# Softcap attention, then a gated feed-forward layer, on one core: VectorE priorities, output copies on VectorE, and weights converted and split one unit further ahead

## Chip, core and metric

The kernel runs on one core of a Trainium2 chip. The metric is the device time of one execution in microseconds (us). TensorE is called PE in the profile, VectorE DVE, ScalarE ACT, GpSimd POOL; SP is SyncE, whose queue (SPq) issues almost all DMAs here.

## What is computed

Attention over 4 batches, 12 heads, 448 positions and 64 features per head, with scores capped by tanh, and then a gated layer whose weights come as 64-bit floats:

```python
def _attn_ref(q, k, v, cap):
    scores = np.matmul(q, k.transpose(0, 1, 3, 2)) / np.sqrt(q.shape[-1])
    scores = cap * np.tanh(scores / cap)
    attn = np.exp(scores - np.max(scores, axis=-1, keepdims=True))
    attn = attn / (np.sum(attn, axis=-1, keepdims=True) + 1e-09)
    return np.matmul(attn, v)

def _moe_ref(x, w_gate, w_val, w_out):   # x: 1792 x 768; w_gate, w_val: 768 x 1536; w_out: 1536 x 768
    gate = 1.0 / (1.0 + np.exp(-(x @ w_gate)))
    return (gate * (x @ w_val)) @ w_out
```

## The kernel before

**Split numbers.** Products are made of halves: a 32-bit value is split into a high part (rounded to the matmul's own format, `hi`, line 171) and a low part (the rest, `lo`, line 180, a subtraction on VectorE at L182), and a product takes three matmuls: high by low, high by high, low by high.

**Attention** works on pairs of heads, numbered n = 0 to 23, six to a batch. `emit_T` (line 285) transposes q and k on TensorE (tiles tp), ScalarE takes the high part T out of PSUM (L176), VectorE the low part. `emit_S` (line 312) makes scores in four pieces sc and ScalarE's tanh takes each out of PSUM (L327); `emit_exp` is the exponential (L335). From pair 12 on, `emit_P` splits it (ph on ScalarE, pl and ph on VectorE) and GpSimd adds it up (tile a); `emit_PV` multiplies with v, and `emit_rd` (line 385) takes the two halves out of PSUM: tmp by ScalarE at L397, then VectorE joins them into xraw at L398. `emit_out` (line 400) divides: reciprocal at L416. Pairs 0 to 11 keep the exponential whole and have no join.

**The layer** runs batch by batch in `moe` (line 706). Weights are cut into 36 units of 128 x 768: units 0 to 23 are w_gate and w_val in three groups of four and four, units 24 to 35 w_out, six for each half t of the output's columns. Batch 0's product with units 0 to 23 makes tiles h (matmuls at L715); with the output units it makes three accumulators o{b}_{t}_0 to o{b}_{t}_2 (L791), 18 matmuls a unit. Accumulators and h share three PSUM buffers. At the end of each half the accumulators are copied into osb: 0 and 2 by VectorE (L804), 1 by ScalarE (L806), and stored.

**Conversion and split.** In batch 0 each unit is made from 64-bit words: `load_w64` (line 601, DMA at L603, a ring of three buffers), `convert_w` (line 606: ScalarE at L620, VectorE at L621, L622 and L623; two buffers in pair0) and `split_w` (line 650: high part by ScalarE at L176, low part by VectorE at L182, into one of four buffers wspl; stored to DRAM as wd at L659). Units 0 to 5 are made during the first six pairs. Later batches load the split units from DRAM (`load_to`, line 665, DMA at L671), into the same four buffers. What is made when is set in `next_w` (line 699), called as TensorE's next unit u is written down:

```python
    def next_w(u):
        if u < NU:
            convert_to(u + LEAD)
        split_w(u + AHEAD)
        load_to(u + WB)
        return w_spl.pop(u)
```

LEAD is 4 and AHEAD 2: with unit u, unit u + 3 is converted and u + 2 is split. A split writes the buffer of the unit four before it.

**The order of work.** TensorE and ScalarE run in the order in which the program writes them down (`manual_schedule`); pieces of attention for the next batch lie between the units. VectorE, GpSimd and SP are ordered by a scheduler, which `high_priority(offset)` tells to place an instruction as if it had been written that many instructions earlier. Only `emit_out`'s division had that before (`AHEAD_OF` is 400).

Of the kernel before, what the change touches and what calls it, by code (L numbers as in the profile page):

```python
# [23 lines left out]
AHEAD_OF = 400  # L24
# [191 lines left out]
def _bounded_attention(o, x_done):  # L216
# [14 lines left out]
    nc, c, ap = o.nc, o.c, o.ap  # L231
# [3 lines left out]
    B, H, S, D, NF, NC, R = o.B, o.H, o.S, o.D, o.NF, o.NC, o.REST  # L235
# [22 lines left out]
    def half(j):  # L258
        return slice(j * D, (j + 1) * D)
# [25 lines left out]
    def emit_T(n):  # L285

        if n >= NP:
            return
        t = qks.pop(n)
        ps = o.two_banks(f"tp{n}")  # L290
        if direct(n):
            o.transpose_evenly(ps[:, 0, :], t[:, 1])
        else:
            for m in range(NC):
                nc.tensor.transpose(
                    ps[:, 0, m * P:(m + 1) * P], t[:, 1, m].rearrange("p h d -> p (h d)"), ident
                )
        o.transpose_evenly(ps[:, 1, :], t[:, 0])
        T[n] = ap.tile([P, 2, 2, BANK], F32R, tag="T", bufs=1, name=f"T{n}")
        w = S if direct(n) else BANK  # L300
        hi, lo = T[n][:, 0, :, 0:w], T[n][:, 1, :, 0:w]
        if direct(n):
            parts = [(hi, lo, ps[:, :, 0:w])]
        else:
            parts = [tuple(
                x.rearrange("p i s -> p (i s)")[:, 0:BANK + S] for x in (hi, lo, ps)
            )]
        for a, b, x in parts:
            o.hi("a", a, x)
            o.lo("v", b, x, a)  # L310

    def emit_S(n, m):

# [65 lines left out]
    def row(n):  # L379
        b, p = divmod(n, o.NPAIR)  # L380
        if b not in x_raw:
            x_raw[b] = o.big.tile([P, o.NPAIR, S], F32, tag="xraw", name=f"xraw{b}")
        return x_raw[b][:, p, :]

    def emit_rd(n, j):

        if direct(n):
            if j == 0:
                rds[n] = ap.tile([P, S], F32, tag="rd", bufs=1, name=f"rd{n}")
            nc.scalar.activation(rds[n][half(j)], pvs[n, j][D:2 * D], AF.Copy)  # L390
            if not alone(n):
                nc.scalar.activation(row(n)[half(j)], pvs.pop((n, j))[0:D], AF.Copy)
        else:

            pv = pvs.pop((n, j))
            tmp = ap.tile([P, S], F32, tag="tmp", bufs=1, name=f"tmp{n}_{j}")
            nc.scalar.activation(tmp[half(j)], pv[D:2 * D], AF.Copy)  # L397
            nc.vector.tensor_add(row(n)[half(j)], pv[0:D], tmp[half(j)])  # L398

    def emit_out(n):  # L400
        b, p = divmod(n, o.NPAIR)
# [155 lines left out]
def _emit(tc, ctx, c, attention_of, q, k, v, w_gate, w_val, w_out, out):  # L557
    nc = tc.nc
    B, H, S, D = q.shape
# [7 lines left out]
    W64 = 3  # L567
    WRAW = 2
    KEEP = 3
    AHEAD = 2  # L570
    WB = 4
    GF = KF // NG

# [4 lines left out]
    o = _Ops(tc, ctx, c, q, k, v)  # L578
# [111 lines left out]
        flush_x()  # L690


    LEAD = 4

    R, NR, KR = o.REST, B * o.REST, 3
    assert NR % P == 0
# [9 lines left out]
    def moe(b):  # L706
        u0 = b * NU
        xs = x_spl[b]

        def passes(ps, s):  # L710
            for kk in range(KD):
                rh, rl = xs[:, 0, kk, :], xs[:, 1, kk, :]
                wh, wl = (s[:, i, kk * P:(kk + 1) * P] for i in range(2))
                for i, (a, r) in enumerate(((wh, rl), (wh, rh), (wl, rh))):
                    nc.tensor.matmul(  # L715
                        ps, a, r, start=(kk == 0 and i == 0), stop=(kk == KD - 1 and i == 2)
                    )
                if kk % 2 == 1:
                    yield 6

        g_spl = big.tile([P, 2, KF, S], F32R, tag="gspl", name=f"gspl{b}")
        rest = []
        if b == B - 1:
            tiles = []
            for tag, bufs, n in o.rest_tags:
                r = ap.tile([P, n, 2, KR, NR], F32R, tag=tag, bufs=bufs, name=f"rest{len(tiles)}")
                tiles += [r[:, i] for i in range(n)]
            for x, r in enumerate(tiles):
                for bb, d in enumerate(g_rest):
                    nc.sync.dma_start(  # L730
                        out=r[:, :, :, bb * R:(bb + 1) * R].bitcast(F32),
                        in_=d[:, :, x * KR:(x + 1) * KR, :].bitcast(F32),
                    )
                rest.append(r)
        u = u0
        for g in range(NG):
            gate = big.tile([P, GF, S], F32, tag="gate", name=f"gate{b}_{g}")
            for which in range(2):
                for j in range(GF):
                    f = g * GF + j  # L740
                    w = next_w(u)
                    u += 1
                    ps = ps_m.tile([P, S], F32, tag="m", name=f"h{b}_{which}_{f}")
                    yield from passes(ps, w)
                    gt = gate[:, j, :]
                    if which == 0:
                        nc.scalar.activation(gt, ps, AF.Copy)  # L747
                    else:
                        nc.vector.tensor_mul(gt, ps, gt)  # L749
                        o.hi("p", g_spl[:, 0, f, :], gt)  # L750
                        o.lo("v", g_spl[:, 1, f, :], gt, g_spl[:, 0, f, :])
                if which == 0:
                    nc.scalar.activation(gate, gate, AF.Sigmoid)  # L753
        moe1_done[b] = True
        flush_x()

        rest_cols = slice(o.FULL, S)
        chunks = [
            lambda i, k, at=m * P: g_spl[:, i, k, at:at + P] for m in range(o.NF)
        ]  # L760
        if b < B - 1:
            d = dram.tile([P, 2, KF, R], F32R, name=f"grest{b}")
            nc.sync.dma_start(out=d.bitcast(F32), in_=g_spl[:, :, :, rest_cols].bitcast(F32))
            g_rest.append(d)
        else:
            for x, r in enumerate(rest):
                for i in range(2):
                    nc.sync.dma_start(
                        out=r[:, i, :, b * R:].bitcast(F32),
                        in_=g_spl[:, i, x * KR:(x + 1) * KR, rest_cols].bitcast(F32),  # L770
                    )
            for at in range(0, NR, P):
                chunks.append(lambda i, k, at=at: rest[k // KR][:, i, k % KR, at:at + P])


        for t in range(2):
            acc = []
            for m in range(len(chunks)):
                if m < o.NF:
                    acc.append(ps_m.tile([P, HM], F32, tag="m", name=f"o{b}_{t}_{m}"))  # L780
                else:
                    acc.append(o.two_banks(f"o{b}_{t}_{m}")[:, 0, 0:HM])
            for x in range(0, KF, KU):
                w = next_w(u)
                u += 1
                for ps, g_of in zip(acc, chunks):
                    for kk in range(KU):
                        wh, wl = (w[:, i, kk * HM:(kk + 1) * HM] for i in range(2))
                        gh, gl = (g_of(i, x + kk) for i in range(2))
                        for i, (a, r) in enumerate(((gh, wl), (gh, wh), (gl, wh))):  # L790
                            nc.tensor.matmul(  # L791
                                ps, a, r, start=(x + kk == 0 and i == 0),
                                stop=(x + kk == KF - 1 and i == 2),
                            )
                    yield 3 * KU * HM / S
            to = out[:, t * HM:(t + 1) * HM]
            osb = big.tile([P, o.NF, HM], F32, tag="gate", name=f"osb{b}_{t}")
            for m, ps in enumerate(acc):
                if m == o.NF:
                    tag, bufs = o.out_tag  # L800
                    osb = ap.tile([P, NR // P, HM], F32, tag=tag, bufs=bufs, name=f"osr{b}_{t}")
                dst = osb[:, m % o.NF, :]
                if m % 2 == 0:
                    nc.vector.tensor_copy(dst, ps)  # L804
                else:
                    nc.scalar.activation(dst, ps, AF.Copy)  # L806
                if m == o.NF - 1:
                    nc.sync.dma_start(
                        out=to[b * S:b * S + o.FULL].rearrange("(m p) e -> p m e", p=P), in_=osb
                    )  # L810
            if b == B - 1:
                ends = to.rearrange("(b s) e -> b s e", s=S)[:, o.FULL:]
                for m in range(NR // P):
                    nb = P // R
                    nc.sync.dma_start(out=ends[m * nb:(m + 1) * nb], in_=osb[:, m, :])
# [7 lines left out]
    with tc.manual_schedule(engines=MS):  # L823
# [6 lines left out]
        for b in range(B):  # L830
            m = moe(b)
# [3 lines left out]
            while live_m or live_a:  # L835
                if live_a and (not live_m or done_a * tot_m <= done_m * tot_a):
                    n = next(att, None)
# [4 lines left out]
                else:  # L842
                    n = next(m, None)
# [34 lines left out]
```

## Time and profile before

| | us |
|---|---|
| median of 3 runs | 802.82 (801.18 to 804.92) |
| the profiled execution | 801.68, its span 799.9 |
| TensorE busy | 754.3 (94%) |
| TensorE weight loads busy | 646.6 (81%) |
| VectorE busy | 469.4 (59%) |
| ScalarE busy | 401.3 (50%) |
| GpSimd busy | 194.5 (24%) |
| mean granted TensorE clock | 0.979 |

Busy times are sums over the span; different stages have different limits, so what bounds the kernel is read stage by stage. The first stage (to 88 us) is attention of batch 0 alone. From 88 to 290 us batch 0's layer runs beside attention of batch 1, and all weights are converted; from 290 to 463 and 463 to 636 us batches 1 and 2 run beside the attention of the next; then batch 3's layer runs alone, until 787.5, and the last 12 us are the last output's way out.

### The profile page before, as it was taken

To read this page: it belongs to the slowest core of one execution; us is meant where nothing else is said; L and a number is where in the kernel's file an instruction comes from. 1 tells how busy PE (TensorE), PEld (TensorE's weight loads), DVE (VectorE), ACT (ScalarE), POOL (GpSimd) and SP (SyncE) were. 2 spreads that over 40 slices of the span, in tenths; PEclk is the share of its full clock that TensorE was granted. 3 is DMA by queue.
4 is the path that set the end of the run, shared out by engine and by line. 5 is a ranking of instruction groups with operands and counts; after the bars stand their busy time and mean duration, and the time that the engine had idled before them with its cause. 6 is when DMAs were issued, how large, how long until landed. Compare 5 with 4: busy or idle time off the path is not lost.

```text
span 799.9 us, 10153 instructions
## 1 busy us (share of the span) xinstructions
PE 754.3 (94%) x3908; PEld 646.6 (81%) x3908; DVE 469.4 (59%) x519; ACT 401.3 (50%) x421; POOL 194.5 (24%) x211
## 2 busy tenths in 40 slices
PE   7999799999998989999999999999979999999993
PEld 5554587888776878988899988887879999999993
DVE  1689349898799926768788628758797011211000
ACT  5898377886766428564764247664741020110000
POOL 1133101020130322524465215344452000100000
PEclk9999899999999989999999999999999999999997
DMA  8777547999989766555557866644378876665531
GB/s 225 179 216 219 181 143 243 363 298 329 289 241 395 246 255 195 179 172 181 174 183 243 276 201 182 193 158 158 127 227 252 289 239 233 211 225 191 180 107 53
DMA packets 133169, 172.99 MB, mean 216 GB/s; under 512 B 86136, under 2 KB 111224, under 8 KB 133112
## 3 DMA queue, kind: packets, MB, share of 16 engines
q1 hardware_dynamic: 132184, 172.02, 67.3%
q8 instruction: 33, 0.54, 0.3%
q10 hardware_dynamic: 928, 0.23, 0.1%
q14 instruction: 24, 0.20, 0.1%
HBM read 135.27 MB, written 36.18 MB: 214 GB/s over the span
## 4 chain that ended last, share of the span: by engine, by line
PE 68%; DVE 14%; ACT 8%; issue 4%; DMA 3%; POOL 1%; SPq 0%; DVEq 0%; POOLq 0%; ACTq 0%
PE h L715 32%; PE o L791 17%; PE pv L365 6%; PE sc L324 5%; DMA w<-in_moe_w_out_dram 2%; DVE pair L623 2%; PE tp L209 2%; ACT t L327 2%; DVE wspl L182 2%; PE pv L374 1%; ACT ph L176 1%; DVE rd L416 1%; PE pv L375 1%; DVE gspl L182 1%; ACT gate L753 1%
## 5 line engine op out<-in xcount | busy, mean ns | idle before, releaser
L715 PE MATMUL h<-xspl,wspl 128*128 128x448 f32 x1728 | 378.5, 373 | 0.0
L715 PEld LDWEIGHTS h<-xspl,wspl 128*128 128x128 f32 x1728 | 322.4, 189 | 42.4 <-issue 15.1
L791 PE MATMUL o<-wspl,gspl 128*128 128x384 f32 x864 | 164.4, 345 | 9.4 <-DVE wspl L182 5.3
L791 PEld LDWEIGHTS o<-wspl,gspl 128*128 128x128 f32 x864 | 154.5, 193 | 14.9 <-DVE wspl L182 5.6
L327 ACT ACTIVATE t<-sc,scale 112x896 f32<-112x896 f32 (+1 forms) x96 | 91.4, 1002 | 17.4 <-PE sc L324 16.8
L747 ACT ACTIVATE gate<-h 128x448 f32<-128x448 f32 x48 | 25.9, 541 | 131.9 <-PE h L715 96.8
L335 ACT ACTIVATE t<-t,capv 112x1792 f32<-112x1792 f32 (+1 forms) x48 | 85.7, 1789 | 0.3
L174 POOL TENSOR_SCALAR gspl<-gate 128x448 fp32r<-128x448 f32 x48 | 34.7, 723 | 206.4 <-DVE gate L749 202.4
L324 PE MATMUL sc<-T 64*112 64x448 f32 (+1 forms) x576 | 75.7, 392 | 9.4 <-DVE T L182 5.6
L365 PE MATMUL pv<-t,vo 112*128 112x448 f32 x192 | 78.6, 542 | 0.0
L324 PEld LDWEIGHTS sc<-T 64*112 64x112 f32 (+1 forms) x576 | 49.6, 183 | 34.6 <-issue 9.3
L416 DVE RECIPROCAL rd<-rd 128x448 f32<-128x448 f32 x24 | 70.7, 2946 | 0.3
L749 DVE TENSOR_TENSOR gate<-h,gate 128x448 f32<-128x448 f32 x48 | 29.6, 616 | 67.8 <-PE h L715 67.5
L806 ACT ACTIVATE osb<-o 128x384 f32<-128x384 f32 x8 | 3.9, 486 | 111.8 <-PE o L791 106.4
L347 POOL TENSOR_TENSOR a<-t 128x448 f32<-128x448 f32 x24 | 30.0, 1251 | 120.1 <-ACT t L335 98.7
L804 DVE COPY osb<-o 128x384 f32<-128x384 f32 x16 | 8.9, 555 | 83.7 <-PE o L791 83.7
L365 PEld LDWEIGHTS pv<-t,vo 112*128 112x128 f32 x192 | 35.4, 189 | 25.2 <-issue 24.7
L182 DVE TENSOR_TENSOR gspl<-gate,gspl 128x448 fp32r<-128x448 f32 x48 | 37.8, 787 | 24.3 <-POOL gspl L174 23.9
L182 DVE TENSOR_TENSOR pl<-t,ph 128x1344 fp32r<-128x1344 f32 x24 | 48.2, 2009 | 4.6 <-ACT ph L176 3.9
L176 ACT ACTIVATE ph<-t 128x1792 fp32r<-128x1792 f32 x24 | 40.7, 1696 | 16.6 <-PE pv L376 8.5
L621 DVE TENSOR_SCALAR pair<-pair 128x768 int32<-128x768 int32 x36 | 21.0, 582 | 42.7 <-ACT pair L620 42.6
L182 DVE TENSOR_TENSOR T<-tp,T 128x896 fp32r<-128x896 f32 (+1 forms) x24 | 26.9, 1121 | 27.3 <-ACT T L176 27.1
(68 smaller groups left out, 758.2 us busy)
## 6 DMA issues: line engine op xcount, KB each, us to landing
wspl<-wd SPq DMA_DIRECT2D x111, 768.0 KB, 4.4
wd<-wspl SPq DMA_DIRECT2D x36, 768.0 KB, 5.3
w<-in_moe_w_gate_dram SPq DMA_DIRECT2D x12, 768.0 KB, 5.2
w<-in_moe_w_val_dram SPq DMA_DIRECT2D x12, 768.0 KB, 7.7
w<-in_moe_w_out_dram SPq DMA_DIRECT2D x12, 768.0 KB, 7.3
qk<-in_q_dram SPq DMA_DIRECT2D x46, 112.0 KB, 4.6
out_dram<-osb SPq DMA_DIRECT2D x8, 576.0 KB, 6.5
qk<-in_k_dram SPq DMA_DIRECT2D x22, 112.0 KB, 4.1
```

Source lines behind the costliest of these rows:

```text
L174: self.nc.gpsimd.tensor_scalar(dst, src, 1.0, 1.0, ALU.mult, ALU.mult)
L176: self.nc.scalar.activation(dst, src, AF.Copy)
L182: e.tensor_sub(dst, src, hi.bitcast(F32))
L324: nc.tensor.matmul(ps[0:w, j, 0:S], a[rows], r[rows], start=(i == 0), stop=(i == len(ops) - 1))
L327: nc.scalar.activation(Pt[n][0:w, :, m, :], ps[0:w, :, 0:S], AF.Tanh, scale=c["scale"][0:w])
L335: nc.scalar.activation(t, t, AF.Exp, scale=c["cap"][rows])
L347: nc.gpsimd.tensor_add(a, t[:, 0, :], t[:, 1, :])
L365: nc.tensor.matmul(pv, vs[n][0:QC, j * NC + m, :], Pt[n][0:QC, j, m, :], start=(m == 0), stop=(m == NC - 1),)
L416: nc.vector.reciprocal(rd, rd)
L715: nc.tensor.matmul(ps, a, r, start=(kk == 0 and i == 0), stop=(kk == KD - 1 and i == 2))
L749: nc.vector.tensor_mul(gt, ps, gt)
L791: nc.tensor.matmul(ps, a, r, start=(x + kk == 0 and i == 0), stop=(x + kk == KF - 1 and i == 2),)
```

## The change

Three things. `LEAD` goes from 4 to 5 and `AHEAD` from 2 to 3: with unit u, unit u + 4 is converted and u + 3 split. The middle accumulator of each half in batches 0 to 2 is copied by VectorE, not ScalarE. And q and k's low parts, the join in `emit_rd` and VectorE's output copies get a high priority with twice the offset. Behind the change, lines from 310 on have numbers higher by 1, from 399 on by 2, from 804 on by 4 (L804 is L808 there, L623 is L625).

```diff
--- before.py
+++ after.py
@@ -307,7 +307,8 @@
             )]
         for a, b, x in parts:
             o.hi("a", a, x)
-            o.lo("v", b, x, a)
+            with o.tc.high_priority(offset=2 * AHEAD_OF):
+                o.lo("v", b, x, a)
 
     def emit_S(n, m):
 
@@ -395,7 +396,8 @@
             pv = pvs.pop((n, j))
             tmp = ap.tile([P, S], F32, tag="tmp", bufs=1, name=f"tmp{n}_{j}")
             nc.scalar.activation(tmp[half(j)], pv[D:2 * D], AF.Copy)
-            nc.vector.tensor_add(row(n)[half(j)], pv[0:D], tmp[half(j)])
+            with o.tc.high_priority(offset=2 * AHEAD_OF):
+                nc.vector.tensor_add(row(n)[half(j)], pv[0:D], tmp[half(j)])
 
     def emit_out(n):
         b, p = divmod(n, o.NPAIR)
@@ -567,7 +569,7 @@
     W64 = 3
     WRAW = 2
     KEEP = 3
-    AHEAD = 2
+    AHEAD = 3
     WB = 4
     GF = KF // NG
 
@@ -690,7 +692,7 @@
         flush_x()
 
 
-    LEAD = 4
+    LEAD = 5
 
     R, NR, KR = o.REST, B * o.REST, 3
     assert NR % P == 0
@@ -800,8 +802,10 @@
                     tag, bufs = o.out_tag
                     osb = ap.tile([P, NR // P, HM], F32, tag=tag, bufs=bufs, name=f"osr{b}_{t}")
                 dst = osb[:, m % o.NF, :]
-                if m % 2 == 0:
-                    nc.vector.tensor_copy(dst, ps)
+                if m % 2 == 0 or b < B - 1:
+
+                    with tc.high_priority(offset=2 * AHEAD_OF):
+                        nc.vector.tensor_copy(dst, ps)
                 else:
                     nc.scalar.activation(dst, ps, AF.Copy)
                 if m == o.NF - 1:
```

What it makes of the order of VectorE's instructions is seen in three places. The first is VectorE at the end of batch 0's first output half, where accumulators o0_0_0 to o0_0_2 are copied. (In names, the number behind the last underscore is a counter; w64_32 holds the words of unit 32, wspl31 is the split of unit 31.) Before:

```order
L621 TENSOR_SCALAR pair0_67<-pair0_67 128x768
L622 SCALAR_TENSOR_TENSOR pair0_67<-w64_31_1882,pair0_67 128x768
L182 TENSOR_TENSOR wspl30_2008<-pair0_67,wspl30_2008 128x768
L623 SCALAR_TENSOR_TENSOR pair0_67<-w64_31_1882,pair0_67 128x768
L804 COPY osb0_0_2081<-o0_0_0_1823 128x384
L621 TENSOR_SCALAR pair0_67<-pair0_67 128x768
L622 SCALAR_TENSOR_TENSOR pair0_67<-w64_32_1913,pair0_67 128x768
L182 TENSOR_TENSOR wspl31_2039<-pair0_67,wspl31_2039 128x768
L623 SCALAR_TENSOR_TENSOR pair0_67<-w64_32_1913,pair0_67 128x768
L804 COPY osb0_0_2081<-o0_0_2_1825 128x384
```

Now:

```order
L623 TENSOR_SCALAR pair0_67<-pair0_67 128x768
L624 SCALAR_TENSOR_TENSOR pair0_67<-w64_32_1893,pair0_67 128x768
L182 TENSOR_TENSOR wspl31_2019<-pair0_67,wspl31_2019 128x768
L625 SCALAR_TENSOR_TENSOR pair0_67<-w64_32_1893,pair0_67 128x768
L808 COPY osb0_0_2090<-o0_0_0_1834 128x384
L808 COPY osb0_0_2090<-o0_0_1_1835 128x384
L623 TENSOR_SCALAR pair0_67<-pair0_67 128x768
L624 SCALAR_TENSOR_TENSOR pair0_67<-w64_33_1924,pair0_67 128x768
L182 TENSOR_TENSOR wspl32_2048<-pair0_67,wspl32_2048 128x768
L625 SCALAR_TENSOR_TENSOR pair0_67<-w64_33_1924,pair0_67 128x768
L808 COPY osb0_0_2090<-o0_0_2_1836 128x384
```

The first copies stand behind the last conversion step of unit 32, where that of unit 31 was, the middle one is new, and the third stands behind unit 33's.

The second place is VectorE a little later, where unit 35 is made. Before:

```order
L182 TENSOR_TENSOR ph12_0_2151<-t12_1953,ph12_0_2151 64x448
L621 TENSOR_SCALAR pair0_67<-pair0_67 128x768
L182 TENSOR_TENSOR wspl34_2183<-pair0_67,wspl34_2183 128x768
L351 TENSOR_TENSOR a12_0_2156<-a12_0_2156 64x448
L415 SCALAR_TENSOR_TENSOR rd11_2056<-rd11_2056 128x448
L182 TENSOR_TENSOR vs13_2290<-v13_2285,vs13_2290 128x8x64
L622 SCALAR_TENSOR_TENSOR pair0_67<-w64_35_2037,pair0_67 128x768
L416 RECIPROCAL rd11_2056<-rd11_2056 128x448
L182 TENSOR_TENSOR as12_0_2161<-a12_0_2156,as12_0_2161 64x448
L623 SCALAR_TENSOR_TENSOR pair0_67<-w64_35_2037,pair0_67 128x768
L421 TENSOR_TENSOR xraw1_812<-xraw1_812,rd11_2056 128x448
L182 TENSOR_TENSOR wspl35_2215<-pair0_67,wspl35_2215 128x768
```

Now:

```order
L623 TENSOR_SCALAR pair0_67<-pair0_67 128x768
L624 SCALAR_TENSOR_TENSOR pair0_67<-w64_35_2017,pair0_67 128x768
L182 TENSOR_TENSOR wspl34_2148<-pair0_67,wspl34_2148 128x768
L625 SCALAR_TENSOR_TENSOR pair0_67<-w64_35_2017,pair0_67 128x768
L182 TENSOR_TENSOR pl12_0_2161<-t12_1964,ph12_0_2160 128x1344
L182 TENSOR_TENSOR ph12_0_2160<-t12_1964,ph12_0_2160 64x448
L182 TENSOR_TENSOR wspl35_2188<-pair0_67,wspl35_2188 128x768
L417 SCALAR_TENSOR_TENSOR rd11_2065<-rd11_2065 128x448
L182 TENSOR_TENSOR vs13_2290<-v13_2285,vs13_2290 128x8x64
L352 TENSOR_TENSOR a12_0_2165<-a12_0_2165 64x448
L418 RECIPROCAL rd11_2065<-rd11_2065 128x448
```

All of unit 35's conversion has moved ahead of pl12_0 (which stood right before ph12_0 in both), and its split ahead of pair 11's division (rd11) and pair 13's v.

The third is VectorE at the end of batch 1's second half. Before, and now:

```order
L421 TENSOR_TENSOR xraw2_2375<-xraw2_2375,rd17_3714 128x448
L182 TENSOR_TENSOR xspl2_3397<-xraw2_2375,xspl2_3397 128x448
L804 COPY osb1_1_3813<-o1_1_0_3677 128x384
L804 COPY osb1_1_3813<-o1_1_2_3679 128x384
L351 TENSOR_TENSOR a18_1_3915<-a18_1_3915 64x448
L182 TENSOR_TENSOR as18_1_3920<-a18_1_3915,as18_1_3920 64x448
```

```order
L182 TENSOR_TENSOR xspl2_3397<-xraw2_2375,xspl2_3397 128x448
L352 TENSOR_TENSOR a18_1_3915<-a18_1_3915 64x448
L182 TENSOR_TENSOR as18_1_3920<-a18_1_3915,as18_1_3920 64x448
L808 COPY osb1_1_3813<-o1_1_0_3677 128x384
L808 COPY osb1_1_3813<-o1_1_1_3678 128x384
L808 COPY osb1_1_3813<-o1_1_2_3679 128x384
```

The three copies now stand behind the two instructions on pair 18's sums. On ScalarE, whose order is the program's, the copy of the middle accumulator is gone, and each conversion and split has the next unit's number. TensorE's order is the same.

## Rows read from the trace of the kernel before

**Rows 1.** Windows by stage: length, busy PE, PEld, DVE, ACT, POOL; clock, DMA, GB/s

```profile
88.00:204.00 116.00, 115.61 (x554) 92.30 (x554) 80.14 (x96) 81.36 (x94) 9.73 (x13) 0.99 0.80 261
204.00:257.00 53.00, 49.13 (x254) 39.92 (x252) 52.08 (x62) 34.72 (x41) 9.34 (x10) 1.00 0.90 303
257.00:290.50 33.50, 27.35 (x131) 24.84 (x131) 25.74 (x27) 14.31 (x17) 8.01 (x7) 0.85 0.74 272
290.50:463.00 172.50, 169.91 (x938) 153.03 (x936) 121.97 (x124) 97.10 (x96) 74.01 (x72) 1.00 0.63 203
```

**Rows 2.** Timeline of PE, end of batch 0: start, length, instructions, [idle before <- releaser]

```profile
251.98 1.31 PE L791 MATMUL o<-wspl,gspl 128*128 128x384 f32 x6
253.51 1.31 PE L791 MATMUL o<-wspl,gspl 128*128 128x384 f32 x6 [0.22 <-DVE osb L804]
257.84 2.29 PE L791 MATMUL o<-wspl,gspl 128*128 128x384 f32 x6 [3.02 <-ACT osb L806]
259.93 1.06 PE L295 MATMUL tp<-ident,qk 128*128 128x128 f32 x4
...
261.27 2.35 PE L791 MATMUL o<-wspl,gspl 128*128 128x384 f32 x12
...
283.44 5.68 PE L791 MATMUL o<-wspl,gspl 128*128 128x384 f32 x18 [5.31 <-DVE wspl L182]
...
290.47 5.12 PE L715 MATMUL h<-xspl,wspl 128*128 128x448 f32 x24
```

**Rows 3.** Timeline of PE, end of batch 2

```profile
598.29 0.44 PE L374 MATMUL pv<-pl,vs 128*128 128x448 f32 x1 [4.43 <-DVE xraw L398]
...
605.96 3.31 PE L791 MATMUL o<-wspl,gspl 128*128 128x384 f32 x18
```

**Rows 4.** Timeline of ACT, end of batch 0 and end of batch 1

```profile
252.86 0.90 ACT L620 ACTIVATE pair<-w 128x768 f32<-128x768 f32 x1 [2.21 <-DMA w<-in_moe_w_out_dram]
...
255.53 1.88 ACT L327 ACTIVATE t<-sc,scale 128x896 f32<-128x896 f32 x2
257.31 0.48 ACT L806 ACTIVATE osb<-o 128x384 f32<-128x384 f32 x1
...
460.84 0.49 ACT L806 ACTIVATE osb<-o 128x384 f32<-128x384 f32 x1 [13.03 <-PE o L791]
```

**Rows 5.** Timeline of DVE, end of batch 0

```profile
251.99 1.03 DVE L623 SCALAR_TENSOR_TENSOR pair<-w,pair 128x768 uint16<-128x768 uint32 x1
...
256.13 1.02 DVE L623 SCALAR_TENSOR_TENSOR pair<-w,pair 128x768 uint16<-128x768 uint32 x1
...
260.94 1.06 DVE L623 SCALAR_TENSOR_TENSOR pair<-w,pair 128x768 uint16<-128x768 uint32 x1
...
267.88 2.51 DVE L182 TENSOR_TENSOR pl<-t,ph 128x1344 fp32r<-128x1344 f32 x1
270.42 1.46 DVE L182 TENSOR_TENSOR ph<-t,ph 64x448 fp32r<-64x448 f32 x1
...
276.79 2.94 DVE L416 RECIPROCAL rd<-rd 128x448 f32<-128x448 f32 x1
...
280.41 1.02 DVE L623 SCALAR_TENSOR_TENSOR pair<-w,pair 128x768 uint16<-128x768 uint32 x1
...
282.34 1.05 DVE L182 TENSOR_TENSOR wspl<-pair,wspl 128x768 fp32r<-128x768 f32 x1 [0.41 <-ACT wspl L176]
```

**Rows 6.** Timeline of SP's queue, a load of 64-bit words

```profile
243.18 0.40 SPq L603 DMA_DIRECT2D w<-in_moe_w_out_dram  x1
```

**Rows 7.** Costliest groups of the page: busy us, mean ns, idle before

```profile
L804 DVE COPY osb<-o 128x384 f32<-128x384 f32 x16 | 8.9, 555 | 83.7 <-PE o L791 83.7
```

**Rows 8.** Timelines of PE, then of ACT, at a split in unit 15

```profile
172.70 4.17 PE L715 MATMUL h<-xspl,wspl 128*128 128x448 f32 x18
...
174.10 0.85 ACT L176 ACTIVATE wspl<-pair 128x768 fp32r<-128x768 f32 x1 [0.48 <-DVE pair L623]
```

**Rows 9.** Windows of 20 us, the one with the densest DMA

```profile
240.00:260.00 20.00, 16.77 (x83) 13.92 (x82) 18.52 (x22) 13.37 (x16) 1.14 (x1) 0.94 1.02 394
```

## The prediction

> **What bounds the kernel now.** I read the stage windows first. TensorE is busy for 115.6 of 116 us while batch 0's first product runs, and for 169.9 of 172.5 us in batch 1; between them, from 204 to 290.5, it idles 3.87 and 6.15 us, and its granted clock falls to 0.85 there [rows 1]. So the place to gain is the end of batch 0, and what TensorE loses there goes straight onto the end, since the stage behind it is all TensorE.
>
> Next the timeline of TensorE in that place [rows 2]. Two waits stand out. **Wait A**: the first output of w_out's second half starts at 253.51 after 0.22 us (VectorE's output copy), the second at 257.84 after 3.02 us, released by ScalarE's output copy. **Wait B**: unit 35 starts at 283.44 after 5.31 us, released by the VectorE half of its split. Both leave a slow clock behind: six matmuls in 2.29 us where the same six took 1.31, and eighteen in 5.68 where eighteen took 3.31 elsewhere [rows 2, 3]. So A costs 3.24 + 0.98 us and B 5.31 + 2.37 us.
>
> Then the two engines that release them. ScalarE reaches its output copy only at 257.31: it stood 2.21 us at unit 32's conversion until the words had landed (252.86), and the tanh pair (255.53) is queued in between [rows 4]. The words were issued at 243.18, so they took 9.6 us [rows 6]. On VectorE, count the last conversion steps (L623) back from unit 35 at 280.41: units 33, 32 and 31 are at 260.94, 256.13 and 251.99 [rows 5]. Unit 35's step is late because the pl and ph instructions and a reciprocal of 2.94 us stand ahead of it; the split's VectorE half ends at 283.39 (282.34 + 1.05) [rows 5].
>
> **The change, part by part.**
>
> *Conversion one unit earlier (LEAD, AHEAD).* No work is added. Unit 6 starts one unit of TensorE's work sooner, in a stretch where VectorE idles 36 us of 116 [rows 1]; from then on each place of the instruction streams handles a unit number higher by one, and all other work keeps its time. One unit takes VectorE at most 4 to 5 us with all that lies between (251.99, 256.13, 260.94) [rows 5], which that idle time covers; without the cover the stretch from 204 to 257, where VectorE is busy 52.1 of 53 us [rows 1], would be later by that much. The loads and stores move with it on SP: the words of unit 33 are issued where those of 32 were, with the same loads of k, q and v ahead of them. So ScalarE still waits for words at 252.86, one unit further on.
>
> *Wait B.* By the new order all of unit 35's conversion stands ahead of the pl instruction, and its split right behind ph. These two keep their time at the earliest, 267.88 to 271.88; with 1.05 us for the split the weights are ready at 272.9 [rows 5]. TensorE came to unit 35 at 278.13 (283.44 less 5.31) [rows 2]; if A gives 3.3 us it comes at 274.8. So B vanishes, with 1.9 us to spare, and its slow clock too: 7.7 us. The bounds are 0 (the split later than before) and 7.7.
>
> *Wait A, output copies on VectorE.* Both first copies stand behind unit 32's L623, which takes the place of unit 31's (251.99 + 1.03), so they end at 253.5 and 254.1 with 0.56 us each [rows 5, 7]. The first output starts at 253.5 as before, the second right behind it at 254.6. Then come the transposes (259.93 before) [rows 2], which need a buffer that ScalarE's first tanh frees: the pair of 1.88 us starts at 255.53, half of it is over at 256.5 [rows 4]. TensorE is there at 255.6, so 0.9 us is left of the wait; the third output's copy lands meanwhile. Saved: 3.24 + 0.98 - 0.9 = 3.3 us. Bounds: 4.2 (ScalarE early too), and -1.3 (rival 1). I take 3.3, since nothing but the copies changes place against other work there. In all six copies of 0.56 us move to VectorE [rows 7], the middle output of each half in batches 0 to 2; they lie beside TensorE's work. At the end of batch 1 the three copies now stand behind two instructions that wait, through GpSimd, for an exp on ScalarE. That exp stood behind ScalarE's copy, which waited 13.03 us for TensorE [rows 4] and is gone from its queue; with so much room I cost this at 0.
>
> *Start of batch 1.* TensorE's first product needs the buffer of the first output of the second half, whose copy now stands behind the reciprocal. That began 4.9 us after the end of ph; three conversion steps of that span are gone and the split of 1.05 came in, so it ends between 278 and 281, the copy 1.8 us later [rows 5, 7]. TensorE would come at 279.5 (274.8, plus the 7.03 us from 283.44 to 290.47, less 2.37 of slow clock) [rows 2]. A wait of 0 to 3 us; I take 0.3, near the early end, as the steps that went were of about 1 us each.
>
> *Priorities for q and k's low parts and the joins.* In batches 1 and 2 none of these instructions changes place. So the 4.43 us that TensorE waits at 598.29 for a join [rows 3] stay: 0, not a gain.
>
> A rule that speaks against the gain: the Trainium skill (DMA: Bandwidth & Descriptors, Where 436 GB/s comes from) names a ceiling of about 435 GB/s for one core's transfers. The trace agrees that it is near: 394 GB/s at a share of 1.02 from 240 to 260 [rows 9]. By that rule an earlier issue there brings nothing, which is rival 1; the sum above needs only the shift that began before 204, where the share is 0.80 [rows 1].
>
> **Sum.** 801.68 (the profiled execution; its span is 799.9) - 7.7 - 3.3 + 0.3 = 791.0. The median of the runs shown, 802.82, lies 1.14 above that execution; I add half of it: **791.5 us**.
>
> **Rivals.**
> 1. *Transfers set the pace.* A unit's words land no earlier than before, so the copies, now behind unit 32, wait until 257.15 and the third, behind unit 33, until 262.0 [rows 5]; TensorE is then 1.3 us later than before at the third output (262.6 for 261.3). B is still saved. For it: 394 GB/s [rows 9], 9.6 us for a load [rows 6]. Against: 0.80 before 204. -7.7 + 1.3: 795.3. Chance 0.12.
> 2. *Unit 35 late all the same.* It has 1.9 us of room, and the instructions around it are stretched (pl 2.51, ph 1.46 us) [rows 5]. If it is 4 to 5 us later, TensorE waits 2 to 3 us and gets up to 2.4 us of slow clock: 795 to 797. With rival 1 on top nearly all is given back: 798 to 802. Chance 0.13, the small half of it with both.
> 3. *The ring of four takes the wait over (slower).* The split of unit u + 3 writes the buffer of u - 1, so ScalarE now waits until TensorE has finished u - 1, where u - 2 was enough. Behind it in its queue stand tanh and evacuations, and VectorE waits for it in order. Where ScalarE is behind TensorE this costs nothing; the narrowest place I found is the split at 174.10, when TensorE's last matmuls of the unit concerned (a third of the eighteen that start at 172.70) end at 173.9, 0.2 us before [rows 8]. In the twelve output units VectorE has under 1 us of idle time in 53 [rows 1], so each wait of 1.3 us there would be TensorE's: 15.6 us against 11, 806. It decides where ScalarE gets ahead of TensorE by more than 0.9 us a unit. Against it: ScalarE is behind TensorE where it counts, waiting for words at 252.86 [rows 4] while TensorE waits for it. Chance 0.06.
> 4. *The change doesn't act*: the split is early, but both waits are set by transfers and stay: 801 to 802. Chance 0.04.
>
> **How the numbers follow.** Forecast 0.65, rivals 0.12, 0.13, 0.06, 0.04. The lower end of the range is the forecast with all 10.0 us of idle time and 3.35 of slow clock gone, 788.3, or 787.5 from the fastest run shown. The upper end takes in rivals 1 and most of 2: 799.5. A measurement of this kernel can tell some 0.5%, 4.0 us, from no change: below 798.8 counts as faster. Forecast, rival 1 and half of 2 give 0.80; the rest of 2 and 4 give 0.13 within; 0.07 slower.
>
> **What would show it.** Right: in batch 0 no TensorE wait on a weight split, none on ScalarE's output copy; a wait of about 1 us at the transposes near 256, released by tanh; batch 1's first product near 280 instead of 290.47; clock near 1.00 from 257 to 280; the 4.43 us still there, some 11 us sooner. Wrong: output copies after 257 (rival 1), a wait on unit 35's split (rival 2), ScalarE's split waiting for TensorE over many units (rival 3); or batch 1 taking longer than its 172.5 us [rows 1], so that the gain is given back later.

## The result, and the profile after

The changed kernel takes **792.39 us** (median of 4 runs, 791.07 to 795.27), the kernel before 803.47 beside it (801.18 to 804.92): a ratio of **0.987 [0.983, 0.991]**. The profiled execution took 791.81 us with a span of 789.5, against 801.68 and 799.9 before.

The stage windows of the kernel after come first, cut at its own boundary (columns as in [rows 1]):

```profile
88.00:204.00 116.00, 115.58 (x556) 92.34 (x555) 83.85 (x101) 82.61 (x97) 9.12 (x12) 0.99 0.83 272
204.00:257.00 53.00, 50.37 (x265) 41.19 (x263) 52.34 (x64) 34.35 (x41) 10.25 (x10) 1.00 0.91 306
257.00:280.00 23.00, 22.94 (x125) 20.53 (x124) 20.38 (x22) 12.99 (x13) 9.26 (x8) 1.00 0.87 305
280.00:452.50 172.50, 170.01 (x938) 153.09 (x937) 126.54 (x130) 96.85 (x94) 77.69 (x75) 1.00 0.65 206
```

The end of batch 0 takes 23 us where it took 33.5, TensorE is busy in 22.94 of them, and the clock is 1.00 instead of 0.85. The first stage shows the price: VectorE is busy 3.7 us more before 204, which is the unit that moved forward, and TensorE does not notice.

TensorE's timeline after, at the places of [rows 2] and of [rows 3], and one more at 546 us:

```profile
251.34 1.31 PE L793 MATMUL o<-wspl,gspl 128*128 128x384 f32 x6
252.89 2.36 PE L793 MATMUL o<-wspl,gspl 128*128 128x384 f32 x12 [0.24 <-DVE osb L808]
256.15 0.66 PE L295 MATMUL tp<-ident,qk 128*128 128x128 f32 x4 [0.90 <-ACT t L328]
...
257.25 2.38 PE L793 MATMUL o<-wspl,gspl 128*128 128x384 f32 x12
...
265.27 11.98 PE L793 MATMUL o<-wspl,gspl 128*128 128x384 f32 x66
277.19 1.49 PE L325 MATMUL sc<-T 64*128 64x448 f32 x12
278.60 5.22 PE L717 MATMUL h<-xspl,wspl 128*128 128x448 f32 x24
...
546.34 0.66 PE L295 MATMUL tp<-ident,qk 128*128 128x128 f32 x4 [1.79 <-ACT t L328]
...
547.15 4.24 PE L717 MATMUL h<-xspl,wspl 128*128 128x448 f32 x12
...
587.50 0.44 PE L375 MATMUL pv<-pl,vs 128*128 128x448 f32 x1 [4.30 <-DVE xraw L400]
```

Wait A is 0.24 us at the copies and 0.90 us at the transposes, wait B is gone (66 matmuls in a row run through it), and batch 1 begins at 278.60 without a wait. The join's wait in batch 2 is still there, 4.30 us.

A useful measure for all that follows is **the stretch**: from the last six matmuls of the first output half to batch 1's first product. It was 290.47 - 251.98 = 38.49 us before [rows 2] and is 278.60 - 251.34 = 27.26 now: 11.23 us less.

VectorE after, at the copies and where unit 35 is made [rows 5]:

```profile
252.30 1.00 DVE L808 COPY osb<-o 128x384 f32<-128x384 f32 x2
...
264.47 1.03 DVE L625 SCALAR_TENSOR_TENSOR pair<-w,pair 128x768 uint16<-128x768 uint32 x1
...
266.64 2.48 DVE L182 TENSOR_TENSOR pl<-t,ph 128x1344 fp32r<-128x1344 f32 x1 [1.14 <-ACT ph L176]
...
270.11 1.80 DVE L182 TENSOR_TENSOR wspl<-pair,wspl 128x768 fp32r<-128x768 f32 x1
...
273.62 2.94 DVE L418 RECIPROCAL rd<-rd 128x448 f32<-128x448 f32 x1
...
277.78 1.01 DVE L808 COPY osb<-o 128x384 f32<-128x384 f32 x2
```

Unit 35's last conversion step is at 264.47 (before: 280.41), ahead of pl, and its split ends at 271.91; TensorE comes to that unit some 3.3 us before 277.19.

ScalarE after [rows 4]:

```profile
247.96 0.92 ACT L622 ACTIVATE pair<-w 128x768 f32<-128x768 f32 x1 [3.54 <-DMA w<-in_moe_w_out_dram]
...
252.44 0.89 ACT L622 ACTIVATE pair<-w 128x768 f32<-128x768 f32 x1 [2.36 <-DVE pair L625]
```

Unit 32 is converted at 247.96 where it was at 252.86; unit 33's place, 252.44, waits in this execution for VectorE and not for words.

### The profile page after: what moved, and what is told of

The parts are those of the page before. It is cut to its first block, busy times and chain, and to the rows that moved or that the text cites. A ratio compares the mean times of both kernels' runs of the same rounds, so it can differ in the third digit from the quotient of the medians.

```text
span 789.5 us, 10148 instructions
## 1 busy us (share of the span) xinstructions
PE 750.8 (95%) x3908; PEld 643.4 (81%) x3908; DVE 472.6 (60%) x525; ACT 398.6 (50%) x415; POOL 198.0 (25%) x211
## 4 chain that ended last, share of the span: by engine, by line
PE 68%; DVE 15%; ACT 8%; issue 4%; POOL 2%; DMA 1%; SPq 0%; DVEq 0%; POOLq 0%; ACTq 0%
PE h L717 32%; PE o L793 19%; PE pv L366 6%; PE sc L325 5%; DVE pair L625 2%; DVE rd L418 2%; PE tp L209 2%; ACT t L328 2%; DVE wspl L182 2%; PE pv L375 1%; PE pv L376 1%; ACT gate L755 1%; DVE gspl L182 1%; ACT ph L176 1%; DVE pair L624 1%
## 5 line engine op out<-in xcount | busy, mean ns | idle before, releaser
L793 PE MATMUL o<-wspl,gspl 128*128 128x384 f32 x864 | 160.5, 340 | 1.1 <-DVE gate L751 0.8
L793 PEld LDWEIGHTS o<-wspl,gspl 128*128 128x128 f32 x864 | 151.8, 189 | 5.8 <-issue 3.5
L808 DVE COPY osb<-o 128x384 f32<-128x384 f32 x22 | 11.8, 553 | 72.6 <-PE o L793 72.5
L623 DVE TENSOR_SCALAR pair<-pair 128x768 int32<-128x768 int32 x36 | 20.6, 573 | 38.7 <-ACT pair L622 37.2
L622 ACT ACTIVATE pair<-w 128x768 f32<-128x768 f32 x36 | 32.5, 902 | 18.0 <-DVE wspl L182 12.1
```

The lines of the kernel that those rows point to most:

```text
L622: nc.scalar.activation(x, top.bitcast(F32), AF.Copy, scale=2.0 ** -112)
L793: nc.tensor.matmul(ps, a, r, start=(x + kk == 0 and i == 0), stop=(x + kk == KF - 1 and i == 2),)
```

## The experiments

**1. The conversion alone.** The kernel before with two numbers changed:

```diff
-    AHEAD = 2
+    AHEAD = 3
-    LEAD = 4
+    LEAD = 5
```

> LEAD 5 and AHEAD 3 alone; output copies stay as before (ScalarE copies the middle one). Theory (two waits in series, A at the output copies, B at unit 35's split): B and its slow clock go, A stays as it was, about 3 us at ScalarE's copy and six matmuls at half rate. So 7.7 us under before and 3.3 over the full change: 795.7 us, ratio 0.990. Rival (the copies carry most of the gain, by keeping ScalarE free): 799 to 801, and a wait on a split still in the trace.

Measured: 798.58 us, ratio 0.9925 [0.9894, 0.9956]. TensorE's timeline of this run:

```profile
253.59 1.31 PE L791 MATMUL o<-wspl,gspl 128*128 128x384 f32 x6
255.31 1.31 PE L791 MATMUL o<-wspl,gspl 128*128 128x384 f32 x6 [0.41 <-DVE osb L804]
259.97 2.29 PE L791 MATMUL o<-wspl,gspl 128*128 128x384 f32 x6 [3.34 <-ACT osb L806]
...
263.53 3.50 PE L791 MATMUL o<-wspl,gspl 128*128 128x384 f32 x12
...
285.99 5.22 PE L715 MATMUL h<-xspl,wspl 128*128 128x448 f32 x24
```

B is gone, as expected, and the stretch is 32.40 us: 6.09 gained, not 7.7. The rest is at A: it waits 0.5 us more (0.41 + 3.34 for 0.22 + 3.02 [rows 2]), and the slow clock lasts longer behind it, 3.50 us for twelve matmuls that took 2.35. Whether the split has to move too is not shown: LEAD 5 with AHEAD 2 was not run (three units would then be converted and not yet split, and pair0 has two buffers).

**2. The copies and priorities alone**, with LEAD 4 and AHEAD 2 as before. The other two priorities of the change are in as well and not printed again:

```diff
-                if m % 2 == 0:
-                    nc.vector.tensor_copy(dst, ps)
+                if m % 2 == 0 or b < B - 1:
+                    with tc.high_priority(offset=2 * AHEAD_OF):
+                        nc.vector.tensor_copy(dst, ps)
```

> The output copies on VectorE alone; LEAD 4 and AHEAD 2 as before. Theory: wait A shrinks to about 1 us, but unit 35's split comes when VectorE's queue lets it, near 283.4 as before; TensorE only comes to it 3.3 us sooner and waits that much longer there (B near 8.5 us). Nothing gained: 803 us, ratio 0.998 to 1.002. Rival (the parts add up): 3.3 us under before, 800, with B near 5 us.

Measured: 803.4 us, ratio 0.9988 [0.9967, 1.001]. TensorE's timeline:

```profile
252.90 1.31 PE L793 MATMUL o<-wspl,gspl 128*128 128x384 f32 x6
255.31 2.36 PE L793 MATMUL o<-wspl,gspl 128*128 128x384 f32 x12 [1.10 <-DVE osb L808]
...
275.59 4.96 PE L793 MATMUL o<-wspl,gspl 128*128 128x384 f32 x18 [2.03 <-DVE wspl L182]
284.29 6.07 PE L793 MATMUL o<-wspl,gspl 128*128 128x384 f32 x18 [3.74 <-DVE wspl L182]
...
291.72 5.13 PE L717 MATMUL h<-xspl,wspl 128*128 128x448 f32 x24
```

The wait on ScalarE's copy is gone (1.10 us are left at VectorE's), and TensorE then waits 5.77 us for the splits of two units instead of 5.31 for one, with slow matmuls behind both. The stretch is 38.82 us, as before. The wait itself grew by 0.5 us only, not to the 8.5 expected; the rest of what A gave went into slow matmuls, 4.96 + 6.07 us for two units where one slow unit took 5.68 and a fast one takes 3.31. So **the two parts don't add up**: the copies give nothing alone (0.1%), the conversion 0.75%, both together 1.3%. The three intervals alone would just allow a sum; the rows decide it. A and B lie in series before the same late unit 35, which TensorE starts 31.4 us after the stretch begins, here (284.29 - 252.90) as before (283.44 - 251.98). With B gone the copies do count: 798.58 in experiment 1, 792.4 in experiment 3.

**3. The whole change without its priorities.** All three `high_priority` blocks taken out; every engine's instructions then stand in the same order as with them.

> The full change without any of its three priorities. Each engine's order of instructions is the same with and without them, so all theories expect the time of the full change, 792.4 us, ratio 0.987; what it differs by is the noise of the comparison. A ratio above 0.992 would mean that the parts of the change are not what the order of the instructions shows.

Measured: 792.4 us, ratio 0.9863 [0.9836, 0.989], the same as the change. TensorE's timeline at the stretch, and at the 546 us place above:

```profile
252.06 1.31 PE L791 MATMUL o<-wspl,gspl 128*128 128x384 f32 x6
254.72 2.35 PE L791 MATMUL o<-wspl,gspl 128*128 128x384 f32 x12 [1.35 <-DVE osb L804]
...
280.25 5.22 PE L715 MATMUL h<-xspl,wspl 128*128 128x448 f32 x24
...
548.78 2.67 PE L715 MATMUL h<-xspl,wspl 128*128 128x448 f32 x12
```

At the 546 us place TensorE waits 1.78 us. The stretch is 28.19 us. The priorities do nothing here. But the stretch isn't the same in every execution, though the order is: ScalarE waits for unit 33's words in this one,

```profile
253.87 0.90 ACT L620 ACTIVATE pair<-w 128x768 f32<-128x768 f32 x1 [1.93 <-DMA w<-in_moe_w_out_dram]
```

and TensorE 1.35 us for the first copies, where it was 0.24. What that says of the prediction comes below.

**4. The split further ahead, the conversion not.** The whole change, but

```diff
-    LEAD = 5
+    LEAD = 4
```

> The full change with LEAD back at 4: AHEAD is 3, so each unit is split at once behind its own conversion, and conversion is no earlier than before. Theory (it is the earlier conversion that counts): VectorE now has to wait for ScalarE's high part, and ScalarE for VectorE's last conversion step, within every unit, with no other unit's step in between; some 1 to 2 us of VectorE's time a unit is lost in a stretch where it is full. TensorE waits for splits in several output units: 803 us, between 797 and 812. Rival (the split's place alone takes wait B away): 792 to 794.

Measured: **847.02 us**, ratio 1.0566 [1.0528, 1.0605]: a miss by 44 us. Two rows show the size, both from 88 to 320 us, where nearly all weights are made: first this run's window, then the same window of the whole change.

```profile
88.00:320.00 232.00, 199.72 (x902) 159.20 (x901) 153.14 (x174) 124.03 (x143) 24.30 (x26) 0.90 0.68 228
```

```profile
88.00:320.00 232.00, 228.54 (x1151) 188.78 (x1150) 182.00 (x212) 153.44 (x172) 42.58 (x44) 1.00 0.82 270
```

TensorE idles 32 us of 232 instead of 3.5, and the granted clock is 0.90 instead of 1.00. Two lines of this run's list of waits (engine, line waited for: us in total, times, longest):

```profile
ACT wspl L176 <- DVE pair L625: 44.7, 14, 6.1
...
ACT wspl L176 <- PE o L793: 21.2, 7, 3.6
```

In the whole change the first is 8.7 us in 5 waits, and the second doesn't occur. Other matmuls than those of o account for 14.5 us more of the split's waits here, in 4. That left two suspects. With LEAD 4 and AHEAD 3, ScalarE converts unit u + 3 and splits that same unit right behind it, so it stands at the split through VectorE's three conversion steps, with everything behind it in its queue ("coupling"). And the split writes the buffer of unit u - 1, which TensorE has only just used ("ring").

**5. The same coupling with the ring as slack as before.** The whole change, but

```diff
-    AHEAD = 3
+    AHEAD = 2
-    LEAD = 5
+    LEAD = 3
```

> The change with LEAD 3 and AHEAD 2: a unit is again split right behind its own conversion on ScalarE, as in e4_split_ahead_only (LEAD 4, AHEAD 3), but the split writes the buffer of the unit four before it as before the change, so the ring of four is as slack as it was. Theory 'coupling' (e4 lost its time because ScalarE stands at the split until VectorE's three conversion steps of the same unit are done, with tanh and PSUM copies queued behind it): as slow as e4 or slower, 840 to 860 us, ScalarE's split waiting for VectorE's L625 in most units from 88 us on (e4: 44.7 us in 14 waits), no wait of ScalarE's split for TensorE. Theory 'ring' (e4 lost its time because the split of u + 3 waits until TensorE is done with u - 1): near the kernel before or a little faster, 792 to 808 us.

Measured: 853.65 us, ratio 1.0601 [1.0572, 1.0631]. Its waits of ScalarE's split:

```profile
ACT wspl L176 <- DVE pair L625: 79.7, 25, 6.3
...
ACT wspl L176 <- PE o L793: 6.1, 2, 3.3
```

With the ring as slack as before the loss is as large as in experiment 4 (the intervals of the two ratios overlap), the split's wait for VectorE nearly twice as long, and its waits for TensorE, of which none was expected, 9.5 us in 3 (3.4 of them for h) instead of 35.7 in 11. So the loss doesn't need the tighter ring. By itself this run doesn't single the coupling out either, since LEAD 3 also converts each unit one unit later than before. Experiment 4 does: it converts as early as experiment 2 (LEAD 4, 803.4 us) and has the ring of the whole change (AHEAD 3, 792.39), and what neither of them has is the split right behind its own conversion. How it reaches TensorE is seen in experiment 4's timelines, VectorE's first, then ScalarE's, then TensorE's:

```profile
123.42 1.01 DVE L625 SCALAR_TENSOR_TENSOR pair<-w,pair 128x768 uint16<-128x768 uint32 x1
```

```profile
124.51 0.84 ACT L176 ACTIVATE wspl<-pair 128x768 fp32r<-128x768 f32 x1 [3.20 <-issue]
...
125.94 0.54 ACT L393 ACTIVATE xraw<-pv 64x448 f32<-64x448 f32 x1
```

```profile
126.53 3.35 PE L366 MATMUL pv<-t,vo 112*128 112x448 f32 x4 [4.97 <-ACT xraw L393]
```

The split starts 0.08 us after VectorE's last conversion step of that unit has ended (124.43), though its wait of 3.20 us is put down to "issue". Two short PSUM copies (0.54 us each) wait behind the split, TensorE needs their buffer for its next pv and stands for 4.97 us, and then four matmuls take 3.35 us that take 1.67 elsewhere. What of the 55 us the ring adds in experiment 4 is not separated.

**6. Can the 4.30 us at 587.5 be had?** In the whole change VectorE makes four low parts of batch 3's x while TensorE runs towards that wait; the join stands behind them and behind work on pair 23. Their row, and TensorE's denominators (dn) of pairs 22 and 23, between which the wait lies:

```profile
578.45 4.25 DVE L182 TENSOR_TENSOR xspl<-xraw,xspl 128x448 fp32r<-128x448 f32 x4
```

```profile
581.58 0.57 PE L410 MATMUL dn<-as,ones 128*128 128x448 f32 x2
...
598.30 0.57 PE L410 MATMUL dn<-as,ones 128*128 128x448 f32 x2
```

This order suggests two ways. The first: pair 22 is joined before pair 23's first exponential is split.

```diff
-            if not direct(n):
+            late = n == NP - 1
+            if not direct(n) and not late:
                 emit_P(n, 0)
...
                 emit_rd(n - 1, 1)
+                if live and late:
+                    emit_P(n, 0)
```

> The change, and for pair 23 the two halves of pair 22 are joined before pair 23's first exponential is split (the program's order; no work differs): ScalarE's tmp and VectorE's join of pair 22's second half move ahead of a23_0, but stay behind the four low parts of x (xspl3) on VectorE. Theory: the 4.30 us that TensorE waits at 587.5 for the join were VectorE's four low parts (some 4.25 us) and the instructions on pair 23 behind them; taking away only the latter gains 0 to 1 us: 791.5 to 792.5 us, ratio to before 0.985 to 0.988, the wait 3.3 to 4.3 us. Rival: the wait was made by the instructions on pair 23 alone: it falls under 1 us, and the time to 788 to 789.

Measured: 793.29 us, ratio 0.9858 [0.9832, 0.9884]: no gain. TensorE's timeline:

```profile
587.83 0.74 PE L375 MATMUL pv<-pl,vs 128*128 128x448 f32 x1 [3.35 <-DVE pl L182]
...
590.61 4.55 PE L796 MATMUL o<-wspl,gspl 128*128 128x384 f32 x18
```

The join is early, and pl of pair 23, now behind it, is late instead. The wait is 0.95 us shorter, but the slow clock now holds for all seven pv matmuls; from dn to dn it is 16.70 us in this run, 16.72 in the whole change.

**7. The same, with batch 3's low parts of x made by GpSimd** in addition:

```diff
-            o.lo("p" if b == 0 else "v", xs[:, 1, p, :], xr[:, p, :], xs[:, 0, p, :])
+            o.lo("p" if b in (0, B - 1) else "v", xs[:, 1, p, :], xr[:, p, :], xs[:, 0, p, :])
```

> As e8_join_first, and batch 3's four low parts of x are made by GpSimd, not VectorE (as batch 0's are). Theory: with both out of the way the join's wait at 587.5 falls from 4.30 to 1 to 2.5 us and the slow clock behind it shrinks: 788.5 to 790.5 us, ratio to before 0.980 to 0.984. Rival: GpSimd's four low parts (1.2 to 2 us each) hold back its adds of pair 23, TensorE waits for those instead: no faster than the change, 791.5 to 794 us.

Measured: 797.01 us, ratio 0.9902 [0.9881, 0.9924]: slower than experiment 6 beside it (794.21 to 797.91 against 790.77 to 796.43) and above what either theory allowed; against the change itself the intervals overlap. From dn to dn it is 19.9 us (16.7 in experiment 6). GpSimd's timeline, then VectorE's:

```profile
584.11 5.45 POOL L182 TENSOR_TENSOR xspl<-xraw,xspl 128x448 fp32r<-128x448 f32 x3
```

```profile
587.12 1.45 DVE L182 TENSOR_TENSOR ph<-t,ph 64x448 fp32r<-64x448 f32 x1
```

Beside GpSimd's subtractions VectorE's own are stretched: ph takes 1.45 us, and 0.62 in the change, at 586.19, where GpSimd idles. TensorE waits 2.52 us for pl, and 3.17 for the next one. The Trainium skill (SBUF — State Buffer, SBUF: two separate sides) says that a VectorE instruction with two SBUF inputs and a GpSimd instruction that reads SBUF can't run together, and the one that starts second waits; the stretched lengths agree with that, though no row shows the waiting itself. How much of the loss is this, and how much GpSimd's own sums for pair 23 being held back, is not separated.

**8. The low parts later, not elsewhere.** The whole change, with batch 3's x split only behind batch 2's first output copies. ScalarE makes the high parts there, since its order is the program's and it holds the low parts back.

```diff
-            o.hi("p", xs[:, 0, p, :], xr[:, p, :])
+            o.hi("a" if b == B - 1 else "p", xs[:, 0, p, :], xr[:, p, :])
...
-        moe1_done[b] = True
-        flush_x()
+        if b != B - 2:
+            moe1_done[b] = True
+            flush_x()
...
+            if b == B - 2 and t == 0:
+                moe1_done[b] = True
+                flush_x()
```

The middle copy of that one half stays on ScalarE.

> The change, and batch 3's x is split only after batch 2's first output half has been copied out: ScalarE (not GpSimd) makes its six high parts, behind its copy of that half's middle accumulator (left on ScalarE there), so VectorE's six low parts, 4.25 us of them ahead of the join now, stand behind the copies. Theory: the join's 4.30 us wait at 587.5 was made by those low parts, and e10 fell short because GpSimd was given them; the join and pl23_0 are done near 583.2, when TensorE arrives: wait under 0.7 us, slow clock behind it (about 1.6 us) gone, and a wait of 0 to 2 us for pl23_1 or its join a little later: 786 to 789 us, ratio to before 0.977 to 0.981. Rival: what e8 showed, each us of wait that goes comes back as slow clock or as the next wait (pl23_1): 791 to 793 us, ratio 0.985 to 0.987.

Measured: **788.77 us**, ratio 0.9804 [0.9775, 0.9832], the fastest version here; the interval lies below that of experiment 3, which is the change without its idle priorities, and touches that of the change. TensorE's timeline, then VectorE's:

```profile
583.15 0.57 PE L410 MATMUL dn<-as,ones 128*128 128x448 f32 x2
...
585.35 0.44 PE L375 MATMUL pv<-pl,vs 128*128 128x448 f32 x1 [0.58 <-DVE xraw L400]
...
586.84 3.31 PE L794 MATMUL o<-wspl,gspl 128*128 128x384 f32 x18
591.48 0.47 PE L375 MATMUL pv<-pl,vs 128*128 128x448 f32 x1 [1.33 <-DVE pl L182]
...
596.15 0.57 PE L410 MATMUL dn<-as,ones 128*128 128x448 f32 x2
```

```profile
604.52 3.29 DVE L182 TENSOR_TENSOR xspl<-xraw,xspl 128x448 fp32r<-128x448 f32 x6
```

The wait falls from 4.30 to 0.58 us and leaves no slow clock behind it (18 matmuls in 3.31 us); 1.33 us come back at pl. From dn to dn it is 13.00 us instead of 16.72, 3.7 less, which is about the difference of the medians (792.4 to 788.8). The six low parts run in 3.29 us at 604.52, where VectorE has nothing else to do. This run also takes the six high parts off GpSimd, which makes sums for pair 23 there; what that alone is worth is not separated.

## Why the prediction was right

The forecast, 791.5, is 0.9 us from the median. Its mechanism holds, with one term that varies from execution to execution and came out close by luck:

- **Wait B: predicted 7.7 us.** Split ready at 272.9 predicted, 271.91 measured; room 1.9 us predicted, about 2.0 measured (66 matmuls end at 277.2, unit 35 is the last 3.3 us). From the transposes' end to batch 1 it was 290.47 - 261.27 = 29.20 us [rows 2] and is 278.60 - 257.25 = 21.35: 7.85 saved. In experiments 3, 6, 7 and 8, whose instructions stand in the same order up to there, it is 21.31 to 21.36.
- **Wait A: predicted 3.3 us**, with 0.9 us left at the transposes for tanh. Measured: 0.90 us left there, and 9.29 us (251.98 to 261.27) have become 5.91: 3.38 saved. In experiments 3, 6, 7 and 8 the same piece is 6.86, 7.48, 6.93 and 5.57 us, so 1.8 to 3.7 are saved; that one trace gives just the predicted 3.3 is luck.
- **Start of batch 1: 0.3 us of wait allowed for, none came.** The reciprocal began at 273.62 and the two copies behind it ended at 278.79, beside the scores (277.19); batch 1 needs the first of them. I had its end between 278 and 281; it was 276.56, since ph ended 1.8 us earlier than I took it and not at its old time.
- **Priorities 0, batch-1-end copies 0, conversion covered:** the join's wait stayed (4.30 for 4.43), experiment 3 shows the priorities' nothing, and TensorE is as busy before 204 as it was. Batch 1's 172.5 us hold 170.01 busy us for 169.91 [rows 1].
- **Rival 1 (transfers set the pace) fell at the price I gave it:** the first copies ended at 253.30, not at 257.15. I had said that ScalarE still waits for words at 252.86, one unit further on. In the change's own trace it doesn't: unit 32's words were there 4.9 us earlier, and the waiting moved to 247.96, though transfers were as dense (403 GB/s from 240 to 260, 394 before [rows 9]). But in experiments 3, 6, 7 and 8 it does: unit 33's conversion waits 1.75 to 1.93 us for words. So the step was right in four executions of five, and the words are not out of the play: TensorE's wait for the first copies is 0.24 us in the change, 1.35, 1.65 and 1.40 in experiments 3, 6 and 7, and none in 8.
- **Rival 3 (the ring) costs nothing in the change:** no wait of ScalarE's split is put down to TensorE there. One of 3.41 us at 221.59, put down to VectorE, is put down to TensorE in experiments 1 and 8 (3.40), so the two end close together; TensorE is busy 50.37 of 53 us around it. I looked at the wrong half: the trouble close by is a split right behind its own conversion (experiments 4 and 5).
- **Three figures are off and decide nothing.** The six matmuls that I let end at 173.9 end at 174.44 in the trace, 0.3 us behind the split's start and not 0.2 ahead of it; in the change that place costs TensorE nothing (115.58 busy us of 116). The fastest run shown gives a lower end of 787.8, not 787.5. And the chances as listed make 0.835, 0.105 and 0.06, where I wrote 0.80, 0.13 and 0.07.

The sum has an accident in it too. The stretch gave 11.23 us and began 0.64 us earlier, yet the spans differ by 10.4. The missing 1.5 us lie at 547.15: after a 1.79 us wait that both kernels have, twelve matmuls took 4.24 us, where the kernel before has 2.71 and experiment 3 2.67. This is a matter of the one execution and not of the change. By the stretches of the five executions in that order (26.93 to 28.79 us) the change gives 9.7 to 11.6 us against the one trace of before; 0.9 us from the median is closer than the working could know.

## What to carry over

Of two waits in a row ahead of the same late tile, the first is worth nothing by itself: find the last one, and remove it together with those ahead of it. On an engine that runs in program order, put another unit's work between the step that asks another engine for something and the step that takes it back; here that one unit of distance is worth more than 50 us. Less urgent work that becomes ready in a bunch was kept off a critical queue here by giving it a later input; a high priority for the join had changed no order, and a neighbouring engine made it slower.

## What was not expected of the hardware

A shorter wait can cost the same: in experiment 6 TensorE stood 3.35 us instead of 4.30, and matmuls at the lower of its two clock levels (1.2 against 2.4 GHz) took all of it back (granted clock 0.62 from 587.83 to 595.00), while in experiment 8 waits of 0.58 and 1.33 us left no slow matmul (1.00 from 585.35 to 590.00). And a wait doesn't decide it alone: the wait of some 1.8 us of which 546.34 is one occurs twice in the traces of before, the change and experiments 1, 2, 3, 6, 7 and 8 (1.61 to 1.79 us), and in 15 of those 16 places the twelve matmuls behind it took 2.67 to 2.72 us, in one 4.24 (granted clock 0.58 there, in the change). Likewise at the copies: behind 1.40 us in experiment 7 twelve matmuls took 2.35 us, behind 1.65 in experiment 6 they took 3.92.
